# w_in loaded whole ahead of two blocks of x, their convolutions in runs two pairs apart, half of w_out scaled by GpSimd

## The chip, the core and the metric

The kernel runs on one core of a Trainium2 chip. The metric is the device time of one execution in microseconds (us); lower is better. The engines are TensorE (PE; PEld is its weight load), VectorE (DVE), ScalarE (ACT), GpSimd (POOL) and SyncE (SP).

## What is computed

A causal depthwise convolution over the sequence, with 7 taps that come from a softmax of `weight` (8 heads), and then a two-layer network with a swish whose slope `beta` is one per hidden channel:

```python
w = softmax(weight)                       # (8, 7)
x_pad = concat([zeros((B, 6, D)), x])     # B, S, D = 8, 4096, 192
out = einsum('hk,bskhg->bshg', w, x_unf)  # seven shifted rows of x_pad, by head
x = out.reshape(B * S, D)                 # 32768 x 192
h = x @ w_in                              # w_in 192 x 2048
g = h * (1.0 / (1.0 + np.exp(-beta * h)))
return g @ w_out                          # w_out 2048 x 192
```

All inputs and the output are float32.

## The kernel before

The tokens are two streams (`s` = 0, 1) of 16384 rows, worked on together. A step is a stretch of rows of both streams: 128, 128, 256, then 256 four times, then 384 and 512. Steps 0 to 2 are an opening of their own; from step 3 on a steady loop follows. For each step the first product (mm1) goes to PSUM tiles `ph`, of which there are two; ACT applies the swish (Silu with scale beta, so that g comes out times beta) and writes `g`; the second product (mm2) reads `g` and `w_out_s`, which is w_out divided by beta (`scale_w_out`, L273, with `rbeta`), in bf16, in 16 chunks of 128 rows.

The 192 rows of w_in are taken as 3 x 64, and 64 rows lie on half of the 128 partitions. `w_in_s` holds them in both halves. In the opening, half `h` holds only the columns of its own half of the 2048: `load_w_in` (L113) fetches them in three pieces of 256, 384 and 384 columns for each half, with a cast to bf16. `copy_w_in` (L116) copies each half's columns over to the other half, in four DMAs; the steady loop, from step 3 on (mm1, L343), reads both.

In the opening, `mm1_pair(i, u)` (L325) makes hidden chunks u and u + 8 of step i: 6 matmuls, then two activations (L329), for u = 0 to 7. We write (i, u) for this pair. A pair needs an empty `ph`. After each pair, `first_tile(i, u)` adds work that prepares the next rows, and then come the mm2 matmuls (L376) that the table `first_mm2` puts there; `cuts` says which chunks.

The first 512 rows are convolved on TensorE, in four blocks of 128 rows of each stream. For block b: `transpose_0` (L215) transposes it into a PSUM bank, `take_0` (L223) copies that into `xr`, `conv_0` (L229) adds up the taps as matmuls with diagonal weights, 14 in all (taps 0 to 3 are 8, taps 4 to 6 are 6), and `evac_0` (L240) scales the sum into `xcp`. Block 0 is step 0, block 1 is step 1, blocks 2 and 3 are step 2. Two pairs of PSUM banks, `pa` and `pb`, serve the blocks in turn. Later rows are convolved on VectorE (L301, L303), the ones of step 3 while step 2 runs.

Every instruction is pinned to its place in program order on its engine. The queue of GpSimd issues 20 DMAs in the opening, in this order: two pieces of w_in for both halves (4), blocks 2 and 3 of x (`load_x0`, L131, cast to bf16), the third piece of w_in (2), w_out as `w_out_f` (L157, 4), the first part of the next tile of x (`xb1`, L159, 2), its second part (L81, 2), and the copies of w_in (4). VectorE's order in the opening is that of the calls: takes and evacuations, with the 16 scalings of w_out put behind the convolutions at (0,5), (0,6) and (1,1).

Of the kernel before, what the change touches and what calls it, by code (L numbers as in the profile page):

```python
# [19 lines left out]
def kernel(  # L20
# [9 lines left out]
    nc = tc.nc  # L30

    B, S, D = x.shape
    H, K = weight.shape
# [3 lines left out]
    NF = F // 128  # L37
    NK = 3
    Q = D // NK
    NS = 2  # L40
# [3 lines left out]
    NB = TILE // 128  # L44

    def pin(ins):

        return tc.keep_in_program_order(ins)
# [28 lines left out]
    def load_x(j, s, b0=0, b1=NB, eng=None):  # L77
        if j not in xf_of:
            xf_of[j] = xf_pool.tile([128, NB, NS, D], FP32, name="xf")
        src = xs[s, TILE * j + 128 * b0:TILE * j + 128 * b1, :]  # L80
        pin((eng or nc.sync).dma_start(out=xf_of[j][:, b0:b1, s, :],  # L81
                                       in_=src.rearrange("(b p) d -> p b d", p=128)))

    def cast_x(j, s, b0=0, b1=NB, eng=None):
        if j not in xbf_of:
            xbf_of[j] = xbf_pool.tile([128, NB, NK, NS, Q], BF16, name="xb")
        pin((eng or nc.vector).tensor_copy(  # L87
            xbf_of[j][:, b0:b1, :, s, :].rearrange("p b k q -> p k b q"),
            xf_of[j][:, b0:b1, s, :].rearrange("p b (q k) -> p k b q", k=NK)))

    def new_xt(j):
        xt_of[j] = xt_pool.tile([128, NK, LEAD + TILE], BF16, name="xt")

    def transpose_x(j, b):
        if j not in xt_of:
            new_xt(j)
        c = LEAD + 128 * b
        pin(nc.sync.dma_start_transpose(
            out=xt_of[j][:, :, c:c + 128],
            in_=xbf_of[j][:, b, :, :, :].rearrange("p k s q -> p (k s q)")))  # L100
# [4 lines left out]
    w_out_f = consts.tile([128, NF, D], FP32, name="w_out_f")  # L105
    w_out_s = consts.tile([128, NF, D], BF16, name="w_out_s")
    w_out_v = moe_w_out.rearrange("(c p) d -> p c d", p=128)

    def half_of(s):
        return slice(64 * s, 64 * s + 64)  # L110

    def load_w_in(s, f0, f1):
        pin(nc.gpsimd.dma_start(out=w_in_s[half_of(s), :, f0:f1], in_=w_in_v[:, :, f0:f1]))  # L113

    def copy_w_in(s, f0, f1):
        pin(nc.gpsimd.dma_start(out=w_in_s[half_of(1 - s), :, f0:f1], in_=w_in_s[half_of(s), :, f0:f1]))  # L116
# [3 lines left out]
    xb0 = consts.tile([128, 2, NS, D], BF16, name="xb0")  # L120
# [7 lines left out]
    HF = F // 2  # L128

    def load_x0(b, eng):  # L130
        pin(eng.dma_start(out=x0[:, b, :, :] if b < 2 else xb0[:, b - 2, :, :],  # L131
                          in_=xs[:, 128 * b:128 * b + 128, :].rearrange("s p d -> p s d")))
# [17 lines left out]
    for f0, f1 in ((0, 256), (256, 640), (640, HF)):  # L150
        for s in range(NS):
            load_w_in(s, HF * s + f0, HF * s + f1)
        if f0 == 256:
            for b in range(2, NB):
                load_x0(b, nc.gpsimd)
    for c in range(0, NF, 4):
        pin(nc.gpsimd.dma_start(out=w_out_f[:, c:c + 4, :], in_=w_out_v[:, c:c + 4, :]))  # L157
    for s in range(NS):
# [14 lines left out]
    def po_banks():  # L173
        return [po_bank(), po_bank()]
# [34 lines left out]
    def transpose_0(bank, src, b):  # L209

        bf = src.dtype == BF16
        t = (bank.bitcast(BF16) if bf else bank)[:, 0:NK * 128].rearrange("p (k t) -> p k t", k=NK)
        v = src[:, b, :, :].rearrange("p s d -> p (s d)").rearrange("p (m k) -> p k m", k=NK)
        for kk in range(NK):
            pin(nc.tensor.transpose(t[:, kk, :], v[:, kk, :], ident_b if bf else ident))  # L215
        return t

    def take_0(t, b, act=False):
        dst = xr[:, :, PAD + 128 * b:PAD + 128 * b + 128]
        if act:  # L220
            pin(nc.scalar.activation(dst, t, AF.Copy))
        else:
            pin(nc.vector.tensor_copy(dst, t))  # L223

    def conv_0(cv, b, k0=0, k1=K):

        for k in range(k0, k1):
            for s in range(NS):
                pin(nc.tensor.matmul(  # L229
                    cv[s][:, 0:NK * 128], diag[half_of(s), k, :, :].rearrange("p s q -> p (s q)"),  # L230
                    xr[half_of(s), :, 128 * b + k:128 * b + k + 128], start=(k == 0), stop=(k == K - 1)))

    def evac_0(cv, b, s, eng, k0=0, k1=NK):
        i, c = place[b]
        src = cv[s][:, 128 * k0:128 * k1].rearrange("p (k t) -> p k t", t=128)
        dst = xc_of[i][:, s, k0:k1, c:c + 128]
        if eng is nc.scalar:
            pin(nc.scalar.activation(dst, src, AF.Copy, scale=rsum))
        else:
            pin(eng.tensor_scalar_mul(dst, src, rsum))  # L240

    new_xt(0)
    pa = po_banks()
    pb = po_banks()
# [4 lines left out]
        make_diag(k)  # L249
    rsum = consts.tile([128, 1], FP32, name="rsum")  # L250
    pin(nc.vector.reciprocal(rsum, tsum))
    for f in range(0, HF, 512):
        for s in range(NS):
            copy_w_in(s, HF * s + f, HF * s + f + 512)
    pin(nc.scalar.activation(scrap, one, AF.Silu))
    b0 = [cv0[:, 0, :], pb[0]]
    conv_0(b0, 0)
# [9 lines left out]
    rbeta = consts.tile([128, NF], FP32, name="rbeta")  # L267
# [1 line left out]
    tapn = consts.tile([128, K], FP32, name="tapn")  # L269
    pin(nc.vector.tensor_scalar_mul(tapn, etap, rsum))  # L270

    def scale_w_out(c):
        pin(nc.vector.tensor_scalar_mul(w_out_s[:, c, :], w_out_f[:, c, :], rbeta[:, c:c + 1]))  # L273


    def conv_ops(i):
# [224 lines left out]
    def first_tile(i, u):  # L501
        if (i, u) == (0, 1):
            conv_0(pb, 1, 0, 4)
        elif (i, u) == (0, 2):
            conv_0(pb, 1, 4, K)
        elif (i, u) == (0, 3):
            t23 = [transpose_0(pa[b], xb0, b) for b in range(2)]
            for b in range(2):
                take_0(t23[b], 2 + b)
            for s in range(NS):  # L510
                evac_0(pb, 1, s, nc.vector)
        elif (i, u) == (0, 5):
            conv_0(pa, 2, 0, 4)
            for c in range(4):
                scale_w_out(c)
        elif (i, u) == (0, 6):
            conv_0(pa, 2, 4, K)
            for s in range(NS):
                evac_0(pa, 2, s, nc.vector)
            for c in range(4, 8):  # L520
                scale_w_out(c)
        elif (i, u) == (1, 0):
            conv_0(pb, 3, 0, 4)
        elif (i, u) == (1, 1):
            conv_0(pb, 3, 4, K)
            for s in range(NS):
                evac_0(pb, 3, s, nc.vector)
            for c in range(8, NF):
                scale_w_out(c)
        elif (i, u) == (1, 6):  # L530
            new_xt(1)
            ts_ = [transpose_0(pb[b], xb1, b) for b in range(2)]
            for b in range(2):
                pin(nc.vector.tensor_copy(xt_of[1][:, :, LEAD + 128 * b:LEAD + 128 * b + 128], ts_[b]))
            pin(nc.vector.tensor_copy(xt_of[0][:, :, TILE + LEAD - PAD:],
                                      xr[:, :, TILE:].bitcast(FP32)))
        elif (i, u) == (1, 7):
            for s in range(NS):
                cast_x(1, s, 2, NB)
            for b in range(2, NB):  # L540
                transpose_x(1, b)
            for j in (2, 3):
                for s in range(NS):
                    load_x(j, s)
# [2 lines left out]

    prs_0 = ((0, 0), (1, 0))
    first_mm2 = {}
    for key, us, cuts in (((0, 0), [(1, u) for u in range(2, 8)], (0, 3, 6, 9, 12, 13, 16)),  # L550
                          ((1, 0), [(2, 1), (2, 2)], (0, 8, 16)),
                          ((0, 1), [(2, 3), (2, 4)], (0, 8, 16)),
                          ((1, 1), [(2, 5), (2, 6), (2, 7)], (0, 5, 10, 16))):
        for (i, u), c0, c1 in zip(us, cuts, cuts[1:]):
            first_mm2[(i, u) + key] = range(c0, c1)

    for i in range(n_steps):
# [16 lines left out]
        for u in range(0, NF, du):  # L574
            us = range(u, u + du)
# [41 lines left out]
```

## Time and profile before

| | |
|---|---|
| median of 4 runs | 686.32 us (685.75 to 686.9) |
| the profiled execution | 686.9 us |
| its span in the profile | 685.1 us |
| PE, ACT, DVE, POOL busy | 680.7, 583.8, 551.4, 14.5 us |
| granted TensorE clock | 1.0 |
| HBM over the span | 78 GB/s |

The profile is of one execution; times in it count from the start of its span. An engine's timeline lists its instructions in order of time as start, duration, engine, line, operation and tiles, with the idle time before them and what ended it in brackets. The chain of waits follows the work that ended last back to what released it at each step. In the DMA part, time to landing counts from the issue. The pairs of the opening run from 8.7 us to about 31 us; the steady loop fills the rest. The issues of GpSimd before, by the timeline and the DMA part:

| issue | starts, us | us to landing |
|---|---|---|
| w_in, first two pieces | 1.72 to 3.71 | 3.8 to 5.0 |
| blocks 2 and 3 of x | 4.33, 5.07 | 4.9, 4.7 |
| w_in, third piece | 5.79, 6.40 | 4.8, 5.0 |
| w_out | 7.02 to 9.29 | 5.5 to 6.8 |
| xb1 | 10.03, 10.73 | 6.4, 7.5 |
| copies of w_in | 12.90, 14.04, 15.25, 16.33 | 8.4, 7.9, 6.9, 6.3 |

### The profile page before, as it was taken

The numbers are of one execution on the slowest core, as the hardware profiler recorded it, in microseconds if no ns is written. First come the engines' busy times: TensorE is split into PE (matmuls) and PEld (weight loads), VectorE is DVE, ScalarE is ACT, GpSimd is POOL, SyncE is SP. The second block draws the span as 40 slices with busy tenths as digits, with TensorE's granted clock in tenths as the row PEclk, the third lists the DMA queues.
The fourth block names the chain that finished last, engine by engine and source line by source line (L and its number), as shares of the span: only waits on it lengthen the run. The fifth ranks groups of instructions, "written<-read, shape, count | busy, mean of one in ns | idle before, by whom it ended". The sixth has DMA issues, their size and how long they took to land.

```text
span 685.1 us, 27210 instructions
## 1 busy us (share of the span) xinstructions
PE 680.7 (99%) x12528; PEld 463.4 (68%) x12528; DVE 551.4 (80%) x886; ACT 583.8 (85%) x585; POOL 14.5 (2%) x26
## 2 busy tenths in 40 slices
PE   9999999999999999999999999999999999999998
PEld 7799887666666666666666666666666666666667
DVE  5999999999988889888889888889888889875112
ACT  6999999888888888888888888888888888888881
POOL 8000000000000000000000000000000000000000
PEclk9999999999999999999999999999999999999999
DMA  9653434454422444423344323344324443220223
GB/s 209 172 133 92 120 101 101 115 117 117 116 71 68 107 111 117 117 53 85 106 112 117 94 68 93 100 118 117 86 57 106 105 117 72 54 54 14 49 48 94
DMA packets 150418, 66.85 MB, mean 98 GB/s; under 512 B 113648, under 2 KB 149696, under 8 KB 150304
## 3 DMA queue, kind: packets, MB, share of 16 engines
q1 hardware_dynamic: 146992, 61.08, 35.0%
q0 software_dynamic: 3168, 3.93, 2.7%
q8 instruction: 98, 1.61, 1.0%
q14 instruction: 16, 0.13, 0.1%
q10 hardware_dynamic: 144, 0.10, 0.0%
HBM read 28.32 MB, written 25.17 MB: 78 GB/s over the span
## 4 chain that ended last, share of the span: by engine, by line
PE 99%; ACT 0%; DVE 0%; issue 0%
PE ph L343 47%; PE po L422 43%; PE po L376 4%; PE ph L325 2%; PE po L460 2%; PE po L229 1%; PE ph L184 0%; ACT gp L329 0%; PE ph L229 0%; PE po L215 0%; PE ph L190 0%; DVE o_sp L382 0%; PE po L263 0%
## 5 line engine op out<-in xcount | busy, mean ns | idle before, releaser
L348 ACT ACTIVATE g<-ph,beta 128x1024 bf16<-128x1024 f32 (+2 forms) x528 | 557.2, 1062 | 80.9 <-PE ph L343 61.8
L343 PE MATMUL ph<-xc,w_in_s 64*64 64x512 bf16 (+3 forms) x5952 | 613.7, 368 | 0.0
L422 PE MATMUL po<-g,w_out_s 64*64 64x512 bf16 (+1 forms) x5568 | 581.2, 372 | 0.0
L343 PEld LDWEIGHTS <-w_in_s 64*64 64x64 bf16 (+1 forms) x5952 | 276.9, 104 | 124.5 <-issue 0.4
L422 PEld LDWEIGHTS <-w_out_s 64*64 64x64 bf16 x5568 | 291.7, 118 | 83.3
L303 DVE SCALAR_TENSOR_TENSOR acc<-xt,tapn,acc 128x512 f32<-128x512 bf16 (+2 forms) x450 | 311.7, 778 | 0.9
L439 DVE STREAM_TRANSPOSE o_sb<-po 128x512 f32<-128x512 f32 (+1 forms) x87 | 77.0, 885 | 111.1 <-PE po L422 111.1
L303 DVE SCALAR_TENSOR_TENSOR xc<-xt,tapn,acc 128x512 bf16<-128x512 bf16 (+2 forms) x90 | 64.5, 779 | 0.2
L87 DVE CAST xb<-xf 128x768 bf16<-128x768 f32 (+1 forms) x62 | 48.7, 828 | 0.0
L301 DVE TENSOR_SCALAR acc<-xt,tapn 128x512 f32<-128x512 bf16 (+2 forms) x90 | 41.5, 491 | 1.1
L376 PE MATMUL po<-w_out_s,g 64*128 64x192 bf16 x512 | 28.3, 243 | 0.0
L376 PEld LDWEIGHTS <-g 64*128 64x128 bf16 x512 | 23.5, 94 | 1.6
L382 DVE COPY o_sp<-po 128x192 f32<-128x192 f32 x28 | 9.0, 351 | 8.5 <-PE po L460 7.3
L325 PE MATMUL ph<-xcp,w_in_s 64*128 64x256 bf16 (+1 forms) x144 | 15.0, 308 | 0.2
L329 ACT ACTIVATE gp<-ph,beta 128x256 bf16<-128x256 f32 x32 | 12.6, 478 | 1.5 <-PE ph L325 1.2
L460 PEld LDWEIGHTS <-g 128*128 128x128 bf16 x128 | 10.5, 98 | 0.4 <-issue 0.4
L460 PE MATMUL po<-w_out_s,g 128*128 128x192 bf16 x128 | 10.7, 246 | 0.0
L329 ACT ACTIVATE g<-ph,beta 128x512 bf16<-128x512 f32 x16 | 9.6, 693 | 0.1
L325 PEld LDWEIGHTS <-w_in_s 64*128 64x128 bf16 x144 | 7.0, 95 | 3.4 <-issue 1.5
L229 PE MATMUL po<-xr,diag 64*128 64x384 f32 x49 | 8.3, 390 | 0.0
L376 PE MATMUL po<-w_out_s,gp 64*128 64x192 bf16 x128 | 7.6, 243 | 0.0
L376 PEld LDWEIGHTS <-gp 64*128 64x128 bf16 x128 | 6.0, 94 | 1.6
(52 smaller groups left out, 60.9 us busy)
## 6 DMA issues: line engine op xcount, KB each, us to landing
xf<-in_x_dram SPq DMA_DIRECT2D x60, 384.0 KB, 4.1
out_dram<-o_sb SPq DMA_DIRECT2D x108, 192.0 KB, 4.6
xt<-xb SPq DMA_TRANSPOSE x122, 3.0
out_dram<-o_sp SPq DMA_DIRECT2D x10, 192.0 KB, 4.1
w_out_f<-in_moe_w_out_dram POOLq DMA_DIRECT2D x4, 384.0 KB, 6.2
out_dram<-o_sb SPq DMA_DIRECT2D x8, 144.0 KB, 4.1
w_in_s<-w_in_s POOLq DMA_DIRECT2D x4, 192.0 KB, 7.4
out_dram<-o_sp SPq DMA_DIRECT2D x8, 96.0 KB, 1.9
```

The lines of the kernel that those rows point to most:

```text
L87: pin((eng or nc.vector).tensor_copy(xbf_of[j][:, b0:b1, :, s, :].rearrange("p b k q -> p k b q"), xf_of[j][:, b0:b1, s, :].rearrange("p b ...
L229: pin(nc.tensor.matmul(cv[s][:, 0:NK * 128], diag[half_of(s), k, :, :].rearrange("p s q -> p (s q)"), xr[half_of(s), :, 128 * b + k:128 * ...
L301: pin(nc.vector.tensor_scalar_mul(a, src, w))
L303: pin(nc.vector.scalar_tensor_tensor(out=xc_of[i][:, k0:k1, o:o + m] if k == K - 1 else a, in0=src, scalar=w, in1=a, op0=ALU.mult, op1=ALU ...
L325: pin(nc.tensor.matmul(ph[:, h, 0:NS * n], w_in_s[half_of(h), kk, ts(fcs[h], 128)], xc_of[i][half_of(h), :, kk, :], start=(kk == 0), stop= ...
L329: pin(nc.scalar.activation(g_at(i, fcs[h])[:, :, 0:n], ph[:, h, 0:NS * n].rearrange("p (s t) -> p s t", s=NS), AF.Silu, scale=beta[:, fcs[ ...
L343: pin(nc.tensor.matmul(ph[m0:m1, s, n * e:n * e + n], w_in_s[half_of(s), kk, 128 * fc + m0:128 * fc + m1], xc_of[i][half_of(s), kk, 0:n], ...
L348: pin(nc.scalar.activation(g_at(i, fc)[:, :, 0:n], ph[:, :, n * e:n * e + n], AF.Silu, scale=beta[:, fc:fc + 1]))
L376: pin(nc.tensor.matmul(po[q][:, 0:D], g_at(i, fc)[r, s, ts(b, 128)], w_out_s[r, fc, :], start=(phase == 0 and fc == 0), stop=(phase == 1 a ...
L422: pin(nc.tensor.matmul(po_of[i, m][half_of(s), 0:n], w_out_s[half_of(r), fc, m:D:NM], g_at(i, fc)[half_of(r), s, 0:n], start=(first and fc ...
L439: pin(nc.vector.transpose(osb_of[i][:, 0:n // L, :, m], po_of[i, m][:, 0:n].rearrange("p (b l) -> p b l", l=L)))
L460: pin(nc.tensor.matmul(po[:, 0:D], g_at(i, fc)[:, s, ts(b, 128)], w_out_s[:, fc, :], start=(fc == 0), stop=(fc == NF - 1)))
```

## The change

The third piece of w_in is issued ahead of blocks 2 and 3 of x. Chunks 8 to 15 of w_out are scaled by GpSimd instead of VectorE; these instructions stand on its queue between the loads and the four copies of w_in. Blocks 2 and 3 of x are transposed one after (0,3) and one after (0,4), and the evacuations of block 1 come ahead of the takes. The two runs of block 2's convolution move from (0,5) and (0,6) to (0,5) and (0,7), those of block 3 from (1,0) and (1,1) to (1,1) and (1,3). VectorE scales chunks 0 to 4 at (0,7) and 5 to 7 at (1,3). The first mm2 matmuls, of step 0, move from the six pairs (1,2) to (1,7) to (1,4), (1,5), (1,7) and (2,0).

```diff
@@ -150,9 +150,8 @@
     for f0, f1 in ((0, 256), (256, 640), (640, HF)):
         for s in range(NS):
             load_w_in(s, HF * s + f0, HF * s + f1)
-        if f0 == 256:
-            for b in range(2, NB):
-                load_x0(b, nc.gpsimd)
+    for b in range(2, NB):
+        load_x0(b, nc.gpsimd)
@@ -249,9 +248,6 @@
-    for f in range(0, HF, 512):
-        for s in range(NS):
-            copy_w_in(s, HF * s + f, HF * s + f + 512)
@@ -269,8 +265,14 @@
-    def scale_w_out(c):
-        pin(nc.vector.tensor_scalar_mul(w_out_s[:, c, :], w_out_f[:, c, :], rbeta[:, c:c + 1]))
+    def scale_w_out(c, eng=nc.vector):
+        pin(eng.tensor_scalar_mul(w_out_s[:, c, :], w_out_f[:, c, :], rbeta[:, c:c + 1]))
+
+    for c in range(NF // 2, NF):
+        scale_w_out(c, nc.gpsimd)
+    for f in range(0, HF, 512):
+        for s in range(NS):
+            copy_w_in(s, HF * s + f, HF * s + f + 512)
@@ -503,30 +505,27 @@
-        elif (i, u) == (0, 3):
-            t23 = [transpose_0(pa[b], xb0, b) for b in range(2)]
-            for b in range(2):
-                take_0(t23[b], 2 + b)
-            for s in range(NS):
-                evac_0(pb, 1, s, nc.vector)
-        elif (i, u) == (0, 5):
-            conv_0(pa, 2, 0, 4)
-            for c in range(4):
-                scale_w_out(c)
-        elif (i, u) == (0, 6):
-            conv_0(pa, 2, 4, K)
-            for s in range(NS):
-                evac_0(pa, 2, s, nc.vector)
-            for c in range(4, 8):
-                scale_w_out(c)
-        elif (i, u) == (1, 0):
-            conv_0(pb, 3, 0, 4)
-        elif (i, u) == (1, 1):
-            conv_0(pb, 3, 4, K)
-            for s in range(NS):
-                evac_0(pb, 3, s, nc.vector)
-            for c in range(8, NF):
-                scale_w_out(c)
+        elif (i, u) in ((0, 3), (0, 4)):
+            if u == 3:
+                for s in range(NS):
+                    evac_0(pb, 1, s, nc.vector)
+            take_0(transpose_0((pa, pb)[u - 3][0], xb0, u - 3), u - 1)
+        elif (i, u) in ((0, 5), (0, 7)):
+            k0, k1 = ((0, 4), (4, K))[u == 7]
+            conv_0(pa, 2, k0, k1)
+            if u == 7:
+                for s in range(NS):
+                    evac_0(pa, 2, s, nc.vector)
+                for c in range(5):
+                    scale_w_out(c)
+        elif (i, u) in ((1, 1), (1, 3)):
+            k0, k1 = ((0, 4), (4, K))[u == 3]
+            conv_0(pb, 3, k0, k1)
+            if u == 3:
+                for s in range(NS):
+                    evac_0(pb, 3, s, nc.vector)
+                for c in range(5, NF // 2):
+                    scale_w_out(c)
@@ -547,7 +546,7 @@
-    for key, us, cuts in (((0, 0), [(1, u) for u in range(2, 8)], (0, 3, 6, 9, 12, 13, 16)),
+    for key, us, cuts in (((0, 0), [(1, 4), (1, 5), (1, 7), (2, 0)], (0, 3, 5, 10, 16)),
                           ((1, 0), [(2, 1), (2, 2)], (0, 8, 16)),
                           ((0, 1), [(2, 3), (2, 4)], (0, 8, 16)),
                           ((1, 1), [(2, 5), (2, 6), (2, 7)], (0, 5, 10, 16))):
```

## The prediction

> **What bounds the kernel now.** I read the totals of the page and its chain first, then the table by stretches over the first 25 us, then the chain of waits between 8 and 24 us, then the timeline of GpSimd.
>
> ```profile
> PE 680.7 (99%) x12528; PEld 463.4 (68%) x12528; DVE 551.4 (80%) x886; ACT 583.8 (85%) x585; POOL 14.5 (2%) x26
> PE 99%; ACT 0%; DVE 0%; issue 0%
> ```
>
> TensorE is busy in 99% of the span and the chain lies on it. An edit of the opening can then only bring or cost what TensorE loses there. The columns of the table by stretches (busy us of PE, PEld, DVE, ACT, POOL) show that ACT is nearly as full:
>
> ```profile
> 10.00:15.00 5.00, 4.95 (x66) 3.92 (x64) 2.89 (x8) 4.57 (x13) 4.17 (x7) 1.00 1.05 321
> 15.00:20.00 5.00, 4.85 (x78) 3.95 (x76) 4.66 (x16) 4.88 (x14) 1.23 (x2) 1.00 1.15 259
> 20.00:25.00 5.00, 4.96 (x78) 3.32 (x74) 4.33 (x12) 4.84 (x12) 0.00 (x0) 1.00 0.22 52
> ```
>
> A busy PE there also covers matmuls that wait in the pipe, so the chain of waits (start, us, what) is the better view:
>
> ```profile
> 11.38 0.36 PE ph L325 x6
> 11.74 0.02 issue
> 11.77 0.85 ACT gp L329 x2
> 12.61 0.04 issue
> 12.65 0.50 PE ph L325 x6
> ...
> 16.67 0.34 PE ph L325 x6
> 17.02 0.53 PE po L229 x6
> ...
> 20.78 0.45 PE po L215 x6
> ...
> 22.00 0.65 PE ph L325 x6
> 22.64 0.04 issue
> 22.68 0.82 PE ph L325 x6
> ```
>
> A pair (u of mm1_pair) costs TensorE 0.34 to 0.36 us behind other work and 0.50 behind a wait; a run of 8 conv matmuls 0.83 (0.72 once, at 15.95), of 6 0.53; six bf16 transposes 0.45; six mm2 matmuls 0.25, so 0.042 each. A pair may start when ACT has emptied the accumulator of the pair two before it, 0.89 us after that pair's first activation (11.77 to 12.65). ACT itself needs 0.725 a pair: in its timeline, stretch by stretch, its pairs start at 17.93, 18.66, 19.37, 20.09, 20.82. From 22.68, pair (2,1), TensorE has no break. So the moment at which (2,1) starts, with 32 mm2 matmuls behind it as now, decides the end. Work between 11.38 and 22.68: 13 pairs x 0.34, pair (2,0) 0.65, the two later conv blocks 2 x (0.72 + 0.53), transposes 0.90, mm2 1.33: 9.8 us in 11.3. So 1.5 us is the most that any reordering can win here.
>
> **The change, part by part.** *Loads.* GpSimd issues the same 20 DMAs. The three pieces of w_in now take 1.72 + 0.75 + 5 x 0.62 = 5.57; the third and fourth block of x start at 5.57 and 6.30 instead of 4.33 and 5.07. Issues that started between 4.33 and 6.40 landed 4.7 to 5.0 us later, so the blocks land by 10.6 and 11.3. Their transposes come at 11.74 and 12.4: hidden with 1.1 us to spare. Landing over 1.1 us later would hold TensorE's queue. The third piece of w_in lands sooner (9.7 instead of 11.4), but is first read at 12.65: worth nothing.
>
> *The order on TensorE.* I step through it with the rows above (P: start on TensorE, A: start on ACT). (0,3): P 11.38, A 11.77, as before. Three transposes instead of six (0.23): to 11.97. (0,4) P 11.97, A 12.50 (before 12.65). Three transposes, to 12.6. On VectorE, two evacuations now stand before the takes: 11.40, 11.93, takes at 12.46 and 12.94 (starts 0.53 and 0.48 apart, 0.55 long, as in the rows at 12.11 to 13.58); the block is ready at 13.02. (0,5) P 12.66, A 13.23; then 8 conv matmuls 13.16 to 13.99. (0,6) A 14.38: ACT loses 0.42. (0,7) at once, 0.44, to 14.79; A 15.11; 6 conv matmuls to 15.33. (1,0) to 15.69, A 15.84. (1,1) waits for ACT: 15.11 + 0.89 = 16.00, to 16.50, A 16.57; 8 conv matmuls to 17.28 (0.78, between the two prices). (1,2) to 17.63, A 17.66; (1,3) to 18.07, A 18.39; 6 conv matmuls to 18.61; (1,4) to 18.96, A 19.12; 6 mm2 to 19.21; (1,5) P 19.28 to 19.76; 4 mm2 to 19.93; (1,6) P 20.01 to 20.49; transposes to 20.94; (1,7) to 21.27; 10 mm2 to 21.69; (2,0) 0.65 to 22.34; 12 mm2 to 22.84; (2,1). Sum: ACT is ahead at (1,7) (21.3 instead of 21.79), but the mm2 matmuls that filled its waits from (1,2) on now stand behind it: 22.84 against 22.68, **+0.16 us**. With every conv run at its low price 0.3 less, with 0.83 at both 0.1 more; the reading errors of some 0.05 per step add up to perhaps 0.4 either way.
>
> *VectorE.* Eight scalings leave it (0.23 each, 1.9 us in the last row below). It had reached the xt copies at 21.10 waiting for the transposes; these end at 20.94 now, so the conv of step 3 starts as early as before. It ends at 30.74 and is read at 31.2: hidden by 0.5.
>
> *GpSimd.* The lines, timeline of POOL and DVE:
>
> ```profile
> 1.10 0.41 POOL L146 TENSOR_SCALAR_AFFINE_SELECT sel<-sel 8x128 f32<-8x128 f32 x1 [0.65 <-DVE sel L143]
> 1.47 0.28 POOL L148 TENSOR_SCALAR_AFFINE_SELECT ident<-ident 128x128 f32<-128x128 f32 x1
> 7.02 3.05 POOL L157 DMA_DIRECT2D w_out_f<-in_moe_w_out_dram  x4
> 14.04 0.62 POOL L116 DMA_DIRECT2D w_in_s<-w_in_s  x1 [0.49 <-DMA w_out_f<-in_moe_w_out_dram]
> 16.33 0.61 POOL L116 DMA_DIRECT2D w_in_s<-w_in_s  x1 [0.47 <-DMA w_out_f<-in_moe_w_out_dram]
> 18.62 1.91 DVE L273 TENSOR_SCALAR w_out_s<-w_out_f,rbeta 128x192 bf16<-128x192 f32 x8
> ```
>
> The last three copies wait for pieces of w_out, those at 15.25 and 16.33 by their times for the third and fourth (issued at 8.55 and 9.29, 6.4 and 6.8 to landing); the scalings wait for the same two pieces, so they start at those times. No GpSimd scaling is in this trace. Its bounds: from below VectorE's 0.23; from above the dearest select, 0.41 for 128 elements, so 0.62 for 192, plus one VectorE scaling (0.30) that it might wait for: 0.92. I take the nearer select, 128 partitions, 0.28 x 1.5 = 0.42. Then chunk 15 is done at 15.25 + 8 x 0.42 = 18.6; at the upper bound 22.6. Chunks 8 and 9 are read at about 21.5, chunks 10 to 15 from 22.34 to 22.8. So it is hidden up to 0.94 each, (22.8 - 15.25) / 8.
>
> Queued behind the scalings are the four copies of w_in, 0.62 each. First issue 18.6 instead of 12.90; they landed 6.3 to 8.4 us after issue, so the first at 25 to 27 and the last, issued at 20.5, by 28.9. mm1 of step 3 reads them first at 31.2. That cover is gone when the first issue is later than 31.2 - 8.4 = 22.8, the same 0.94 each. Nothing else is queued on GpSimd.
>
> The Trainium skill, SBUF — State Buffer, section "Who interferes with whom", says that a VectorE operation in a two-port mode, or with two SBUF inputs against a GpSimd read, and a GpSimd operation exclude each other for a whole instruction. The trace has an issue of 0.62 at 14.04 beside VectorE scalings (14.10 to 15.16), as long as those beside none. By the rule as an estimate, the five scalings at 16.4 hold GpSimd for 1.2 us: done at 19.8 instead of 18.6, still in time. The GPSIMD Engine Reference, section "Performance versus the Vector engine", has VectorE about twice as fast; as an estimate 0.46 to 0.60 each, done at 18.9 to 20.1, also in time.
>
> **The sum.** Span 685.1 + 0.16; the profiled execution took 686.9, so 1.8 lies around the span, and 687.06 is the time to set against it. Its own time is 0.58 above the median of 686.32, so 686.5.
>
> **Rivals.** *A, the forecast:* a wash; 685.8 to 687.1.
> *B, a real gain:* ACT's lead of 0.4 at (1,7) is kept, because the late mm2 matmuls slip between the halves of (2,0). For it: at 13.84 to 14.3 matmuls of a pair and of a conv run interleave in the rows. Against it: from (2,0) on TensorE is full. It gives 0.4 to 1.0 less, 685.4 to 685.9; to pass 0.2% (1.4 us) nearly all of the 1.5 us of waits must go.
> *C, slower:* GpSimd late, at mm2 of (2,0). It decides from 0.94 us a scaling. At 1.2 chunk 15 is done at 24.85, 2.1 after its need: 688.4; the copies would be late by no more than that. For it: two selects are all there is of GpSimd arithmetic, and a GpSimd span is rough. Against it: both lie far below.
> *D, slower by the VectorE queue:* GpSimd holds VectorE. The five scalings at 16.4 would each wait once: at 0.42, done at 16.4 + 5 x 0.65 = 19.65 instead of 17.55, the evacuations of the fourth block start 1.0 late, chunks 5 to 7 are done at 21.5 for 21.27: +0.3. At 0.92 they are done at 23.9: +2.6, 688.9.
>
> **How the numbers follow.** About 0.2%, 1.4 us, is what a measurement of this kernel can tell from no change. A 0.58, B 0.14, C 0.20, D 0.08. Faster by over that: half of B, 0.07. Slower: most of C and D, 0.24. Within: 0.69. The range takes B's lower end and C up to 1.2 us a scaling: 685.4 to 688.4, leaving out a little below and the worst of C and D.
>
> **What would show it.** Right: transposes of the blocks of x at about 11.8 and 12.4 with no wait for a DMA; eight POOL scalings from 15.3 at about 0.4, ended by 20; the copies issued between 18.6 and 21.1; ACT's (1,7) near 21.3 and TensorE's (2,1) near 22.8; no wait of mm1 L343 for w_in_s at 31. Wrong: a scaling of over 0.9 us, mm2 in (1,7) or (2,0) released by POOL or late DVE scalings, a wait for a copy of w_in in step 3, or (2,1) at 22.2 or sooner.

## The result, and the profile after

The changed kernel takes 686.98 us (median of 33 runs, 686.32 to 687.59), the kernel before 686.19 (53 runs, 685.34 to 687.14): ratio 1.0011, interval 1.0006 to 1.0015. It is 0.8 us slower. The profiled execution took 687.35 us with a span of 685.6, 0.5 above the span of before.

The page's shares of the chain, of the changed kernel:

```profile
PE 93%; DVE 4%; issue 1%; DMA 1%; SPq 1%; ACT 0%; DVEq 0%
```

Before, it was PE at 99%. Now a part of the chain leaves TensorE. Its beginning, from the chain of waits (start, us, what; conv_0 is L228 here, transpose_0 L214, mm1_pair L327):

```profile
11.40 0.34 PE ph L327 x6
11.74 0.28 PE po L214 x3
...
14.41 0.02 issue
14.44 1.58 ACT gp L331 x4
16.02 0.04 issue
16.06 0.50 PE ph L327 x6
...
21.55 0.84 DVE xb L87 x2
...
23.31 0.41 SPq L98
```

The opening on TensorE is as it was stepped through: transposes at 11.74, (1,1) at 16.06 (predicted 16.00) behind ACT. Pair (2,1) starts at 22.79; before it was 22.68, predicted 22.84. But the chain that ends last does not run through it. It goes over VectorE's casts (21.55), SyncE's transposes, the loads of x (xf) and VectorE's convolution, and comes back to TensorE only here (same view, later window):

```profile
23.77 2.24 SPq L98
...
26.05 0.82 SPq L81
...
26.91 5.66 DMA xf<-in_x_dram
...
62.68 0.63 DVE xc L305
63.31 0.14 issue
63.44 0.67 PE ph L345 x6
```

What started it is on GpSimd's timeline:

```profile
15.55 5.96 POOL L269 TENSOR_SCALAR w_out_s<-w_out_f,rbeta 128x192 bf16<-128x192 f32 x8 [2.40 <-DMA w_out_f<-in_moe_w_out_dram]
21.47 2.52 POOL L116 DMA_DIRECT2D w_in_s<-w_in_s  x4
```

Eight scalings take 5.96, 0.745 each, where 0.42 was taken; they end at 21.5, where the prediction named 20 as the latest for being right. The copies go out at 21.5 to 24, instead of 12.9 to 16.9, and meet SyncE's work. SyncE's timeline, before and then after:

```profile
22.64 2.58 SPq L98 DMA_TRANSPOSE xt<-xb  x2
25.25 2.23 SPq L81 DMA_DIRECT2D xf<-in_x_dram  x4
```

```profile
22.42 3.58 SPq L98 DMA_TRANSPOSE xt<-xb  x2
26.05 3.00 SPq L81 DMA_DIRECT2D xf<-in_x_dram  x4
```

The part on DMA issues has these two transposes landing after 2.5 us before and 6.8 after; the loads behind them were issued 0.8 later. VectorE then waits for x, twice, and TensorE once, at the first 384-row step (timelines of DVE and PE after):

```profile
31.34 0.85 DVE L87 CAST xb<-xf 128x768 bf16<-128x768 f32 x1 [0.51 <-DMA xf<-in_x_dram]
32.59 0.85 DVE L87 CAST xb<-xf 128x768 bf16<-128x768 f32 x1 [0.41 <-DMA xf<-in_x_dram]
63.44 0.67 PE L345 MATMUL ph<-xc,w_in_s 64*128 64x384 bf16 x6 [0.35 <-DVE xc L305]
```

So of this profile's 0.44 on TensorE (its last 128 matmuls start at 671.53 instead of 671.09) 0.11 is the new order's and about 0.35 stands behind the late copies (whether they are the cause is tested below). The medians, though, are 0.8 apart, and the profile of before was of one of its longer runs, 686.9. Where the rest of the 0.8 comes from was the second question for the experiments.

### The profile page after: what moved, and what is told of

It reads as the page before. It is cut to its first block, busy times and chain, and to the rows that moved or that the text cites. A ratio compares the mean times of both kernels' runs of the same rounds, so it can differ in the third digit from the quotient of the medians.

```text
span 685.6 us, 27210 instructions
## 1 busy us (share of the span) xinstructions
PE 680.7 (99%) x12528; PEld 461.0 (67%) x12528; DVE 550.5 (80%) x878; ACT 583.7 (85%) x585; POOL 20.5 (3%) x34
## 4 chain that ended last, share of the span: by engine, by line
PE 93%; DVE 4%; issue 1%; DMA 1%; SPq 1%; ACT 0%; DVEq 0%
PE ph L345 45%; PE po L424 43%; DVE acc L305 2%; PE po L462 2%; DMA xf<-in_x_dram 1%; PE po L378 1%; PE ph L327 1%; DVE o_sp L384 1%; PE po L228 1%; DVE acc L303 1%; PE ph L183 0%; SPq L98 0%; PE ph L228 0%; DVE xb L87 0%; PE po L214 0%
## 5 line engine op out<-in xcount | busy, mean ns | idle before, releaser
L327 PE MATMUL ph<-xcp,w_in_s 64*128 64x256 bf16 (+1 forms) x144 | 14.3, 309 | 0.4 <-ACT gp L331 0.2
L239 DVE TENSOR_SCALAR xcp<-po,rsum 128x384 bf16<-128x384 f32 (+2 forms) x8 | 4.2, 562 | 6.1 <-PE po L228 6.1
L327 PEld LDWEIGHTS <-w_in_s 64*128 64x128 bf16 x144 | 6.5, 95 | 3.6 <-issue 1.3
L228 PE MATMUL po<-xr,diag 64*128 64x384 f32 x49 | 7.9, 388 | 0.0
```

The costliest lines, as they stand in the source:

```text
L327: pin(nc.tensor.matmul(ph[:, h, 0:NS * n], w_in_s[half_of(h), kk, ts(fcs[h], 128)], xc_of[i][half_of(h), :, kk, :], start=(kk == 0), stop= ...
```

## The experiments

Ratios are to the kernel before, with their 95% intervals; where a text speaks of medians, it is to the median of before in the same batch. Ratios of less than 0.1% (0.7 us) lie near what can be told apart, and several intervals below are wide enough to hold two of the rival forecasts. Labels such as e1 are those that the quoted expectations use. The code is shortened to the lines that matter.

**One part alone: GpSimd's (e1).** In the kernel before:

```diff
-    copies of w_in behind the loads
-            for c in range(8, NF):
-                scale_w_out(c)
+    for c in range(NF // 2, NF):
+        scale_w_out(c, nc.gpsimd)
+    copies of w_in
```

> The kernel before with only the GpSimd part of the change: chunks 8 to 15 of w_out scaled by GpSimd, the four copies of w_in behind them; the order of convolutions and mm2 as before. Theory T (the late copies share the DMA engines with SyncE's transposes and loads of x, VectorE gets x late, and TensorE waits at the first 384-row step): copies issued at about 21 to 24, VectorE waits about 0.9 us in sum for xf at 31 to 33, TensorE waits 0.2 to 0.5 us at 63, pair (2,1) starts at 22.7 as before; time 0.4 to 0.8 us above before. Rival O (the new order on TensorE costs it): the time of before, within 0.2 us.

687.52, ratio 1.0020 (1.0011 to 1.0028). The late copies do what T says, more strongly: VectorE waits 1.17 and 0.36 for xf at 32 to 33, and TensorE waits. But its timeline has more:

```profile
20.99 0.26 PE L379 MATMUL po<-w_out_s,gp 64*128 64x192 bf16 x2 [0.45 <-POOL w_out_s L270]
21.80 0.26 PE L379 MATMUL po<-w_out_s,gp 64*128 64x192 bf16 x2 [0.55 <-POOL w_out_s L270]
64.06 0.66 PE L346 MATMUL ph<-xc,w_in_s 64*128 64x384 bf16 x6 [0.61 <-DVE xc L306]
```

The scalings are late for mm2 too, which was not expected. In this run the first pair started at 7.03, not 8.72: TensorE was ahead by 1.7, and ran into GpSimd, which was done at 21.7, about when it was in the changed kernel.

**One part undone: the scalings back on VectorE (e2)**, the copies early, the new orders kept:

```diff
-    for c in range(NF // 2, NF):
-        scale_w_out(c, nc.gpsimd)
+            if u == 5:
+                for c in range(4):
+                    scale_w_out(c)
-                for c in range(5):
+                for c in range(4, 11):
-                for c in range(5, NF // 2):
+                for c in range(11, NF):
```

> The changed kernel with all 16 scalings on VectorE (chunks 0 to 3 at (0,5), 4 to 10 at (0,7), 11 to 15 at (1,3)) and so the copies of w_in early, at 13 to 17: the new order alone. T: no wait of VectorE for xf, none of TensorE at 63; pair (2,1) at 22.8; time 0 to 0.3 us above before. O: 0.6 to 0.9 us above before, as the change.

687.0, ratio 1.0006 (0.9998 to 1.0015). No wait for xf and none at 63, and (2,1) at 22.84, as T has it; but the time is 0.8 above before by the medians, as O has it and as in the changed kernel, so late copies seem not to be all (the interval holds both forecasts). Again the first pair started early, at 7.10, and TensorE's timeline shows what it met:

```profile
9.90 0.39 PE L325 MATMUL ph<-xcp,w_in_s 64*128 64x256 bf16 x4 [0.90 <-DMA w_in_s<-in_moe_w_in_dram]
...
11.89 0.35 PE L214 MATMUL po<-ident_b,xb 128*128 128x128 bf16 x3 [0.61 <-DMA xb<-in_x_dram]
```

**The copies by another queue (e3):** in `copy_w_in`, `nc.gpsimd` becomes `nc.sync`.

> The changed kernel with the four copies of w_in issued on SyncE's queue, which is idle until 22.4, instead of behind the scalings: they go out when w_in has landed, at 8 to 12. The scalings stay on GpSimd. T: the transposes of SyncE land after 2.5 us again instead of 6.4 to 7.1, no wait for xf, none at 63; time 0 to 0.3 us above before, if w_out does not land over 1 us later beside the copies. Rival G (the GpSimd scalings themselves, at 0.745 each and with VectorE's slowed from 0.23 to 0.4 beside them, cost it): 0.6 to 0.9 us above before.

690.59, ratio 1.0054 (1.0039 to 1.0069): a miss of both. No wait for xf; but the copies, issued from 7.77 on, share the DMA engines with w_out and x. The third piece of w_out released the scalings at 17.31 instead of 15.55, and xb1 came so late that TensorE waited 2.16 for its transposes at 22.14. The condition in the expectation (w_out at most 1 us later) failed. In the changed kernel's profile the DMA engines are full from 4 to 17 us (a busy share of 0.95 or more); with these copies among the loads they stayed full until 20. What is put there pushes something else. The profile is of one of the two shortest of its six runs, 688.44; what the others met, some 2 to 3 us more, it doesn't show.

**The copies ahead of the scalings on GpSimd (e4):**

```diff
-    for c in range(NF // 2, NF): scale_w_out(c, nc.gpsimd)
     copies of w_in
+    for c in range(NF // 2, NF): scale_w_out(c, nc.gpsimd)
```

> The changed kernel with the copies ahead of the scalings on GpSimd's queue. T: copies at 13.2 to 17, scalings 17.2 to 23.2; no wait for xf and none at 63, but chunk 15 is done 0.4 to 0.6 after the mm2 matmuls of (2,0) want it, so (2,1) starts at 23.2 to 23.4; time 0.5 to 0.8 us above before by that other place. G: the same loss at the same place as the change, (2,1) at 22.8.

688.8, ratio 1.0034 (1.0021 to 1.0047). The loss moved to the place that T names, but was larger: the copies took until 17.9, the scalings 17.95 to 24.45, and the mm2 matmuls of (2,0) waited 1.1 in sum, so that (2,1) started at 24.59. No wait for xf, none at 63.

```profile
23.77 0.26 PE L378 MATMUL po<-w_out_s,gp 64*128 64x192 bf16 x2 [0.66 <-POOL w_out_s L269]
```

**The load order alone (e8)**, in the kernel before (w_in whole, then the two blocks of x), and **the load order undone (e5)**, in the changed kernel. W is the theory that runs differ in the moment at which TensorE's matmuls get faster, and that after an early start it is held up by the loads; C is that the late copies are all of the loss:

> The kernel before with only the new load order: w_in whole, then the third and fourth block of x. Before transposes both blocks behind (0,3), at 10.3 in an early start. W: 0.3 to 0.8 us above before; in an early start the profile shows TensorE waiting for xb. C: the time of before, within 0.2 us.

> The changed kernel with only the load order undone: the third and fourth block of x ahead of the third piece of w_in again. New theory W: where TensorE's matmuls reach full speed at 4.5 us instead of 8 (the first pair then starts at 7.3 instead of 8.7), the blocks of x, landing at 11 to 12 by the new load order, hold the transposes of (0,3) and (0,4); the late copies cost their 0.4 besides. W: 0.2 to 0.6 us below the changed kernel, 0.3 to 0.6 above before; no wait of TensorE for xb in a profile with an early start. Rival C (the late copies are all of the loss): the time of the changed kernel, 0.7 above before.

The load order alone: 687.12 (686.37 to 687.22), ratio 1.0008 (0.9999 to 1.0016), 0.9 above before by the medians and 0.5 by the ratio, near W's 0.3 to 0.8; C's 0.2 lies inside the interval too. Its first pair started at 7.28, and TensorE lost the lead at once:

```profile
9.80 0.39 PE L324 MATMUL ph<-xcp,w_in_s 64*128 64x256 bf16 x4 [0.62 <-DMA w_in_s<-in_moe_w_in_dram]
...
11.80 0.35 PE L214 MATMUL po<-ident_b,xb 128*128 128x128 bf16 x3 [0.61 <-DMA xb<-in_x_dram]
12.38 0.35 PE L214 MATMUL po<-ident_b,xb 128*128 128x128 bf16 x3 [0.24 <-DMA xb<-in_x_dram]
```

The first of these waits, and the one of 0.90 in e2, is not for the blocks of x. It is at (0,2), for the second piece of w_in, which is issued at 3.7 in either order. It landed at 9.2 to 9.9 in the seven profiles with the new load order and at 8.2 to 9.3 in the seven with the old one. So the new order seems to delay this piece too, by what now follows it at once; no run tests that by itself.

Undoing the load order was a miss: 687.51, ratio 1.0015 (1.0006 to 1.0023), not below the changed kernel. With x in time TensorE reaches mm2 sooner than GpSimd is done: in its profile (first pair at 8.13) the chain at (2,0) runs through GpSimd's scalings, and (2,1) comes 0.2 late for it. One wait gives its place to the next. But this profile is of one of its shorter runs, 686.7, and why others reach 688 to 689 stays open.

**The order on TensorE alone (e6)** (old load order, all scalings on VectorE as above):

> Load order as before and all scalings on VectorE (chunks 0 to 3 at (0,5), 4 to 10 at (0,7), 11 to 15 at (1,3)), copies early: of the change only the order on TensorE and of the mm2 matmuls is left. W: within 0.3 us of before. Rival O (the new order itself costs): 0.5 us or more above before.

686.77, ratio 1.0004 (0.9995 to 1.0012): 0.5 above before by the medians, as O has it, 0.3 by the ratio, as W has it, so undecided. Its profile has an early first pair (7.17) and two waits of TensorE, 0.88 for the third piece of w_in and 0.44 behind VectorE, whose scalings, as placed in this experiment, waited for w_out. So the old load order has its price in an early start too: the third piece, which landed at 12.22, is the one that is then late. What the order costs in an early start stays open.

**Second profiles** of both kernels, unchanged:

> The kernel before, once more, for a second profile. Theory W says that its times split by the moment at which TensorE's matmuls get faster: with the first pair at about 8.7 us the time is 686.9 to 687.1, with it at 7.3 us the time is 685.4 to 686.2 and pair (2,1) starts 0.8 us or more before 22.68. Against W: an early first pair and a time near 687.

> The changed kernel, once more, for a second profile. W: with an early first pair (7.3 us) TensorE waits for the third piece of w_in or the blocks of x at 9 to 12, (2,1) starts no sooner than 22.4, and the time stays above 686.3; with a late one it is as in the first profile. Against W: an early first pair without such waits.

Before: 686.01, first pair at 7.82, (2,1) at 21.78, both 0.9 sooner than in the first profile, and the time 0.9 less. The matmuls of the first convolution show the moment (PE timeline of this run):

```profile
5.94 0.52 PE L229 MATMUL ph<-xr,diag 64*128 64x384 f32 x1
6.25 0.40 PE L229 MATMUL ph<-xr,diag 64*128 64x384 f32 x1
6.49 0.33 PE L229 MATMUL ph<-xr,diag 64*128 64x384 f32 x1
```

The same matmul takes 0.52 and then 0.33 us. In the first profile all seven took 0.52 or more; the granted clock is 1.00 throughout in both. After: 687.09 with a late first pair (8.70), (2,1) at 22.79; SyncE took 4.06 to issue its two transposes and they landed after 5.6 and 4.7, but VectorE waited only 0.2 for xf and TensorE not at all at 63. So in a late start the late copies cost from nothing to 0.35. The changed kernel was not caught in an early start, so what it loses there is inferred from the kernels that have a part of the change.

**No early starts (e9 from before, e10 from the changed kernel):** in both `warm(9, 256)` becomes `warm(1, 128)`.

> The kernel before with eight of its nine first warm-up matmuls taken out and the ninth cut to 128 columns, so that TensorE gets faster later in every run: no early starts. W: first pair at 8.7 us or later; median 0.6 to 1.5 us above before; no time under 686.5.

> The changed kernel with the same cut of the warm-up. W: the blocks of x have landed when TensorE wants them, so what is left of the loss is the late copies and the order: 0 to 0.5 us above e9 (medians), where the changed kernel is 0.8 above before. Rival (the loss doesn't depend on the start): again 0.7 to 0.9 above e9.

Before: 686.74, ratio 1.0002 (0.9993 to 1.0011); after: 686.80, 1.0008 (0.9999 to 1.0017). The medians are 0.06 apart instead of 0.8, as W has it, but the intervals overlap, and the cut did not do what it was for: three of the eleven runs of before were still under 686.5, its first pair came at 8.48, and its median rose by 0.4, not by 0.6 or more. It speaks for W without settling its size.

**A better order (e7):** convolutions of blocks 2 and 3 in runs of two taps behind each pair, with VectorE's scalings and the cuts of mm2 spread to match, the rest as in e6:

```diff
+        elif (i, u) in ((0, 5), (0, 6)):
+            conv_0(pa, 2, 2 * u - 10, 2 * u - 8)
+            for c in range(4 * u - 20, 4 * u - 16):
+                scale_w_out(c)
+        elif (i, u) == (0, 7):
+            conv_0(pa, 2, 4, 6)
+        elif (i, u) == (1, 0):
+            conv_0(pa, 2, 6, K)
...
+            conv_0(pb, 3, 0, 1)
+        elif (i, u) in ((1, 1), (1, 2), (1, 3)):
+            conv_0(pb, 3, 2 * u - 1, 2 * u + 1)
...
-    (0, 3, 5, 10, 16)
+    (0, 4, 8, 12, 16)
```

> As e6, but the convolutions of blocks 2 and 3 in runs of two taps (4 matmuls, some 0.41 us) behind each pair from (0,5) to (1,3), and 4 chunks of mm2 at each of (1,4), (1,5), (1,7) and (2,0). A run of 4 fits beside a pair (0.34 + 0.41 = 0.75 against ACT's 0.725), so ACT should lose nothing from (0,5) on: (2,1) at 21.9 to 22.1 in a late start instead of 22.7 to 22.8; time 0.3 to 0.8 us below before. If VectorE or the loads of x decide instead (they land at 19 to 20.5 whatever the order), within 0.2 us of before.

685.94 (685.04 to 686.19), ratio 0.9988 (0.9980 to 0.9997): it beats both kernels: its median is 0.3 below that of before, at the low end of what was expected, and 1.0 below the changed kernel's. Its profile has an early start, so the forecast for (2,1) in a late one was not tested. Its pairs run at ACT's pace without a gap, 0.73 apart, from 13.53 on (PE timeline):

```profile
14.26 0.50 PE L326 MATMUL ph<-xcp,w_in_s 64*128 64x256 bf16 x6
14.51 0.62 PE L229 MATMUL po<-xr,diag 64*128 64x384 f32 x4
14.99 0.50 PE L326 MATMUL ph<-xcp,w_in_s 64*128 64x256 bf16 x6
```

All profiles together (us; the last column is the start of the last 128 matmuls minus that of (2,1)):

| kernel | first pair | (2,1) | between | rest |
|---|---|---|---|---|
| before | 8.72 | 22.68 | 13.96 | 648.41 |
| before again | 7.82 | 21.78 | 13.96 | 648.41 |
| before, warm-up cut | 8.48 | 22.43 | 13.95 | 648.42 |
| after | 8.74 | 22.79 | 14.05 | 648.74 |
| after again | 8.70 | 22.79 | 14.09 | 648.39 |
| after, warm-up cut | 8.54 | 22.59 | 14.05 | 648.39 |
| load order alone | 7.28 | 22.88 | 15.60 | 648.42 |
| GpSimd's part alone | 7.03 | 22.52 | 15.50 | 649.63 |
| scalings on VectorE | 7.10 | 22.84 | 15.74 | 648.39 |
| copies by SyncE | 8.18 | 24.47 | 16.29 | 648.39 |
| copies first | 8.82 | 24.59 | 15.77 | 648.39 |
| x early | 8.13 | 22.43 | 14.30 | 648.45 |
| order alone | 7.17 | 22.71 | 15.54 | 648.39 |
| short runs | 7.15 | 21.18 | 14.03 | 648.39 |

In a late start the change costs 0.1 between the first pair and (2,1). Before keeps a lead of 0.9 to the end. The kernels with the new load order, with GpSimd's scalings or with the new order on TensorE lose such a lead: (2,1) is never sooner than 22.4 with any part of the change but the short runs. This also fits that the parts don't add: GpSimd's alone 1.3, loads alone 0.9 and order alone 0.5 (medians) would make 2.7, the whole costs 0.8. If each wait uses up the same lead, that is what comes.

In the 53 runs of before, 14 lie at 686.90 to 687.14 and 39 at or below 686.57, none between. No run of the changed kernel is under 686.32. In the batches of the experiments single runs of before do lie between, at 686.72 and 686.82. By the two profiles the upper group are the latest starts, which is inferred from them and not counted. The changed kernel's median of 686.98 lies in that upper group: against late starts of before it is a wash, and the 0.8 is mostly what before wins in its other runs and the changed kernel does not.

## Why the prediction was right, and where not

The time lies in the range, the sign is that of the sum, and a wash within 0.2% is what came. But of the 0.8 us the forecast reason, the order on TensorE, brought about 0.1. The rest, as far as the experiments show it, lies in terms that the sum put at nothing, the loads and the copies, and that the total still lay inside a range of 3 us is in part luck.

- *The order on TensorE, +0.16.* Right in a late start, for which it was worked out: (2,1) at 22.79 for 22.84, 0.09 to 0.14 more between the first pair and (2,1) in each of the three profiles than in those of before, and the single steps within 0.1.
- *"The blocks land by 10.6 and 11.3 ... hidden with 1.1 us to spare."* This step failed. They landed at 11.2 and 11.8 in the first profile after (5.6 and 5.5 to landing, where 4.7 to 5.0 was taken), and the need at 11.74 was read from a profile of a late start. In an early one it comes 1 us sooner or more. With the load order alone this shows as 0.61 and 0.24 of waiting for the blocks, and 0.62 for the second piece of w_in, which the prediction left where it was. The sentence said what would happen with 1.1 us less; it did not ask whether other runs have that. The same holds for the third piece, "worth nothing" because first read at 12.65: in the early start of e6 it was wanted 0.88 before it had landed.
- *GpSimd's scaling, 0.42 each.* 0.745, inside the bounds of 0.23 and 0.92, but done at 21.5 instead of 18.6. Rival C's limit of 0.94 held for a late start; in an early one the limit is lower, and the GpSimd part alone shows waits of 0.45 and 0.55.
- *"That cover is gone when the first issue is later than 22.8."* The copies were in time for mm1 of step 3, at 21.47. But only their own reader was asked, not who shares the DMA engines: SyncE's transposes went from 2.5 to 6.8 us and its loads of x were late. It cost 0.35 in one profile and nothing in two others. Where the copies went out early (e2, e3, e4) the transposes landed after 2.3 to 2.6 again, with GpSimd's scalings still there in e3 and e4: so it is the copies.
- *VectorE, rival D.* GpSimd does slow VectorE: five scalings beside it took 1.97, at steps near 0.4 (D had 0.65); with the copies by SyncE, where GpSimd's come later, the same five took 1.23, at 0.23. GpSimd's own stayed at 0.74 to 0.76 a step in the profile after, but four of them took 0.82 to 0.94 with the copies first, while VectorE scaled, copied and cast. So the interference that the Trainium skill describes (SBUF — State Buffer, "Who interferes with whom") shows here, but not as an exclusion for a whole instruction: VectorE's steps grew by 0.1 to 0.2, where one of GpSimd's instructions lasts 0.745. The estimate drawn from the rule, GpSimd held for 1.2 us, did not come in the changed kernel. No stall of TensorE followed from it there. And the factor of about two of the GPSIMD Engine Reference ("Performance versus the Vector engine"), measured there on an addition of two tensors, is 3.2 here, 0.745 to 0.23. DVE timeline of the copies by SyncE, then of after:

```profile
15.82 1.23 DVE L269 TENSOR_SCALAR w_out_s<-w_out_f,rbeta 128x192 bf16<-128x192 f32 x5
```

```profile
16.35 1.97 DVE L269 TENSOR_SCALAR w_out_s<-w_out_f,rbeta 128x192 bf16<-128x192 f32 x5
```

## What to carry to other kernels

A slack read from one profile holds for that run's start. Where the times of a kernel fall into groups, look at which group the profile belongs to before calling a load hidden, and ask what the other group would do with the slack. A transfer that is moved later is not only late for its reader: see who else uses the DMA engines then. And several small losses in an opening don't add: each can take from the same lead, so that undoing one may win nothing.

## What was not expected of the hardware

TensorE's matmuls change from 0.52 to 0.34 us at a moment that differs from run to run: before 5.3 us in the profile of e2, at 6.25 in the second of before, after 7.2 in the first. The first pair starts at 7.03 to 8.82 over all the profiles. The Trainium skill (TensorE: Matmul & The Clock Gate, "Part 1: The HAM clock gate") has a free-running window of about 3.4 us that must be busy before the clock doubles, and a change that shifts by 0.5 us either way; these profiles show a wider shift, over 2 us, and a granted clock of 1.00 on both sides of it. Whether that gate is what changes here, they don't show.

Copies within SBUF landed after 3.0 to 6.5 us when issued at 21.5 to 24, and after 6.3 to 8.4 when issued at 12.9 to 16.3 among the loads; transposes issued beside the former took 6.4 to 7.1 us to land in the first profile after, and 4.7 to 5.6 in the second, instead of 2.3 to 2.6.

GpSimd's issues of DMAs also wait where no data asks for it. In the first profile of before the last three copies of w_in, which don't read w_out, go out at 14.04, 15.25 and 16.33, each 0.3 after a piece of w_out has landed (13.8, 15.0, 16.0), and each time that piece is the DMA eight issues back in the queue. The prediction read these waits as marks of when w_out has landed, which they are, though not because the copies need it.
